# A three-stage attention and gated-MLP kernel: the half pair in the first group of the sixth-stage products, the second group run backward, four weight sets converted later and in place

## The chip, the cores and the metric

The kernel runs on one core of a Trainium2 chip. The core has five engines with a queue each: PE (TensorE, matmuls; PEld is its weight load), DVE (VectorE), ACT (ScalarE), POOL (GpSimd) and SP (SyncE, which here issues nearly all DMAs). The metric is the device time of one execution in microseconds (us), less is better.

## What is computed

Attention over 32 learned slots (8 batches, 8 heads, 576 tokens, 64 wide), then a gated MLP, then a squared-ReLU MLP:

```python
x = attention(q, k, v, phi)                    # 4608 tokens x 512
xn = x / sqrt(mean(x * x) + 1e-6) * rms_g
y = (silu(xn @ w_gate) * (xn @ w_val)) @ w_out1   # 512 -> 1536 -> 512
h = maximum(y @ w_in2, 0) ** 2                 # 512 -> 2048
out = h @ w_out2                               # 2048 -> 512
```

## The kernel before

Every fp32 product is made of three fp32r matmuls: each operand is split into a high part (a rounded copy, ACT) and a low part (the rest, DVE or POOL), and high x high, high x low and low x high are summed in PSUM. The helper `split` (L76) does this; it is the line behind most ACT rows (L79) and DVE or POOL rows (L88, and L100 where the low part is put off to the next piece).

**Phase A** (`phase_a`, L886) makes attention and the gated MLP, batch by batch, 24 items (n) a batch: an item is half a batch (288 tokens) by 128 of the 1536 hidden columns. PE makes g and v (6 matmuls each), ACT makes Silu of g (`sl`, L898), DVE multiplies by v, ACT and POOL split the product (`uh`, `ul`), and two items later PE multiplies it by `w_out1` into y (24 matmuls an item in all). g has one PSUM bank: PE cannot begin g of item n+1 before ACT has read g of item n. Each item has four slots, a (after g), b (after v), c (after `uh`), d (after the products into y), where other work is put in program order.

**The last batch** (items 168 to 191) has no next batch's attention to prepare. There the slots from n = 171 on take one piece each from a list (`last_batch`, L921). The pieces prepare the last MLP, which is made by a Strassen-like scheme of 7 products for 8: `x2` pieces (seven each for two halves kk of the tokens of one pair) make the seven sums of y blocks, split; `w2` pieces make the seven sums of a weight block: two pieces with sums on POOL (`w2_sums`), three that split 256, 512 and 1024 columns (`w2_split`, parts a, c, b; ACT, then DVE). A finished weight set is 128 x 3584 fp32 (1792 KB) and is stored to DRAM (`wd`). The input of a set is 512 KB (two DMAs, into `xr`, which has two buffers, and from there the next is loaded when the last piece of a set has run). There are eight sets of `w_in2` ("i", q = 0 to 7) and eight of `w_out2` ("z"). In the last batch all eight z sets and i sets 0 and 1 are made.

**Phase H** (`phase_h`, L1140) makes h. A step is a pair of token blocks by a set q: seven products, 42 matmuls, 512 columns wide (256 in the half pair, pair 4), with four results `c` that are squared and stored to `gd`. `c` has six buffers. Pairs 0 and 2 keep their sums in the `x0` tiles, 1 and 3 in `x1`, the half pair in `x4`. The order of the steps is written out in `STEPS` (L42): group 0 has pairs 0 and 1 (A, B), group 1 pairs 2, 3 and 4 (A, B, C), both with q from 0 up. `h_plan` (L1085) tells which pieces and loads go with which step. In group 0 the i sets 2 to 7 are made, stored, and all eight are loaded again (`Wr`, L1006) for group 1, in three slots `wi0`, `wi1`, `wi2`, the load a step to three ahead of its use. In the last steps of group 1 the eight z sets are loaded (`T`, L1013) into the freed `x0` and `x1` tiles.

**Phase Z** (`phase_z`, L1247) makes out: 72 sums g, 42 matmuls each, from the z sets and from sums S of h. For each g, `s_load` loads two blocks (`sr`, 2 x 256 KB), `s_sums` adds on DVE and POOL, `s_split` makes S (1792 columns: ACT 1.7 us, DVE 2 us) in the `wi` slots. S of g = 0 and 1 are made in group 1; `sr` of g = 2 goes into `x4_1`, that of g = 3 into `xr`. Every four sums share four PSUM accumulators; the first four take the banks y0 to y3.

The DMAs of SP go out in program order, and land about in that order when the queue is full.

Of the kernel before, what the change touches and what calls it, by code (L numbers as in the profile page):

```python
# [9 lines left out]
F32 = mybir.dt.float32  # L10
# [44 lines left out]

TOK = (0, P, HALF - P)
# [8 lines left out]
class Kernel:  # L65
# [88 lines left out]
    def run(self):  # L154
# [43 lines left out]
        with tc.manual_schedule():  # L198
            self.phase_a(NI * (B - 1) + 3, NI * B + 1)
# [721 lines left out]
    def last_batch(self):  # L921
# [61 lines left out]
    def w2_split(self, kind, q, slot, part):  # L983
# [101 lines left out]
    def h_plan(self):  # L1085
# [3 lines left out]
        def at(g, name, pieces, *loads):  # L1089
            p = 2 * g + "ABC".index(name[0])  # L1090
# [8 lines left out]
        def w2(q):  # L1099
            return self.w2_pieces("i", q, q % 3)  # L1100
# [10 lines left out]
        at(0, "B1", w2(3), wl(5))
        at(0, "A3", w2(4), xl(4, 0))
        at(0, "A4", w2(5), wl(6))
        at(0, "B3", x2(4, 0), xl(4, 1))
        at(0, "A5", w2(6), wl(7))
        at(0, "B4", x2(4, 1), xl(2, 0))
        at(0, "A6", w2(7), xl(2, 1))
        at(0, "B5", x2(2, 0, 0, 5))
        at(0, "B6", x2(2, 0, 5), xl(3, 0))
        at(0, "B6", x2(2, 1, 0, 3))  # L1120
        at(0, "B7", x2(2, 1, 3), xl(3, 1))
        at(1, "A0", x2(3, 0, 0, 5))
        at(1, "A1", x2(3, 0, 5), partial(self.s_load, 0))
# [229 lines left out]
```

## Time and profile before

| | |
|---|---|
| median of 3 runs | 1628.73 us (1628.13 to 1630.13) |
| profiled execution | 1628.44 us, span of its instructions 1626.7 us |
| busy: PE, DVE, ACT, POOL | 94%, 63%, 45%, 39% |
| chain that ended last | PE 72%, DVE 8%, DMA 6%, ACT 5%, POOL 4% |
| HBM read, written | 208.28 MB, 101.84 MB |

Times in the rows are counted from the start of the span. Phase A ends near 886 us, its last batch takes about the last 110 us of it; phase H runs from 886 to 1242, its group 1 from 1045; phase Z from there to the end. PE is the engine that does the work, so the question at each place is what it waits for, and which of its two clock levels was granted. A busy PE in the profile includes some waiting, since the ends of matmuls are modelled.

### The profile page before, as it was taken

The page shows a single profiled execution, that of the slowest core. Times are in us where ns is not written, and L with a number is a line of the kernel's source. Part 1 is how long each engine was busy: PE and PEld are TensorE (multiplying, and loading weights), DVE is VectorE, ACT ScalarE, POOL GpSimd, SP SyncE. Part 2 cuts the span into 40 slices and gives each one's busy share as a digit, 9 for nine tenths or more (in the row PEclk, how much of TensorE's full clock was granted, in tenths as well). Part 3 has the DMA queues.
Part 4 walks back from the last instruction along what each step waited for, and adds up shares of the span by engine and source line. Part 5 has one row for each costly group of instructions (what it writes and reads, how often), then busy time and mean ns, then how long its engine had stood idle before and what let it go on. Part 6 is the DMA issues. An engine that isn't in the chain of part 4 may idle for free.

```text
span 1626.7 us, 29659 instructions
## 1 busy us (share of the span) xinstructions
PE 1530.5 (94%) x11594; PEld 1353.6 (83%) x11594; DVE 1016.8 (63%) x1548; ACT 733.0 (45%) x1304; POOL 639.6 (39%) x637
## 2 busy tenths in 40 slices
PE   6687999999999999999878999999998899999998
PEld 3465798888989888898877788878887899999998
DVE  5755645656464565635644777776654777777874
ACT  2656535354443545434543656664443333333332
POOL 0475534344344434424564513430000444444442
PEclk7788999999999999999989999999998899999999
DMA  9897583764758374313496577866479444444442
GB/s 264 278 313 257 205 231 137 211 197 148 189 188 230 132 216 145 111 52 132 151 345 227 196 257 266 265 205 232 164 249 333 144 130 130 138 138 134 135 130 69
DMA packets 207388, 312.07 MB, mean 192 GB/s; under 512 B 31664, under 2 KB 151472, under 8 KB 197008
## 3 DMA queue, kind: packets, MB, share of 16 engines
q1 hardware_dynamic: 203360, 307.56, 58.4%
q10 hardware_dynamic: 3824, 2.49, 0.6%
q8 instruction: 91, 1.49, 0.4%
q14 instruction: 49, 0.40, 0.1%
q0 software_dynamic: 64, 0.13, 0.0%
HBM read 208.28 MB, written 101.84 MB: 191 GB/s over the span
## 4 chain that ended last, share of the span: by engine, by line
PE 72%; DVE 8%; DMA 6%; ACT 5%; POOL 4%; issue 4%; SPq 0%; DVEq 0%; POOLq 0%; ACTq 0%
PE z L1277 7%; PE z L1275 7%; PE z L1276 7%; PE y L868 5%; PE y L869 5%; PE y L870 5%; PE v L852 3%; PE h_S L1082 3%; PE h_S L1083 3%; PE h_S L1081 3%; PE wp L571 3%; PE g L852 3%; PE v L853 2%; PE v L854 2%; PE g L853 2%
## 5 line engine op out<-in xcount | busy, mean ns | idle before, releaser
L88 POOL TENSOR_TENSOR ul<-sl,uh 128x288 fp32r<-128x288 f32 x192 | 168.7, 879 | 365.8 <-ACT uh L79 361.4
L1275 PE MATMUL z<-T,S 128*128 128x256 f32 x1008 | 286.8, 285 | 12.8 <-ACT S L79 6.0
L1277 PE MATMUL z<-T,S 128*128 128x256 f32 x1008 | 286.1, 284 | 1.3 <-DVE S L88 1.3
L1276 PE MATMUL z<-T,S 128*128 128x256 f32 x1008 | 286.0, 284 | 0.0
L868 PE MATMUL y<-uh,woh 128*128 128x288 f32 x768 | 237.1, 309 | 0.0
L869 PE MATMUL y<-uh,wol 128*128 128x288 f32 x768 | 229.1, 298 | 0.0
L870 PE MATMUL y<-ul,woh 128*128 128x288 f32 x768 | 227.9, 297 | 0.0
L79 ACT ACTIVATE S<-sr 128x1792 fp32r<-128x1792 f32 x72 | 122.6, 1703 | 205.4 <-PE z L1277 141.4
L902 DVE TENSOR_TENSOR sl<-sl,v 128x288 f32<-128x288 f32 x192 | 86.0, 448 | 199.4 <-PE v L854 141.0
L1275 PEld LDWEIGHTS z<-T,S 128*128 128x128 f32 x1008 | 195.2, 194 | 13.5 <-ACT S L79 6.2
L1277 PEld LDWEIGHTS z<-T,S 128*128 128x128 f32 x1008 | 194.1, 193 | 1.6 <-DVE S L88 1.6
L1276 PEld LDWEIGHTS z<-T,S 128*128 128x128 f32 x1008 | 194.2, 193 | 0.0
L88 DVE TENSOR_TENSOR S<-sr,S 128x1792 fp32r<-128x1792 f32 x70 | 144.0, 2057 | 55.8 <-ACT S L79 55.8
L1231 POOL TENSOR_TENSOR sr<-sr 128x256 f32<-128x256 f32 x72 | 84.1, 1168 | 232.3 <-DVE sr L1228 232.3
L868 PEld LDWEIGHTS y<-uh,woh 128*128 128x128 f32 x768 | 146.6, 191 | 18.0 <-issue 17.2
L79 ACT ACTIVATE uh<-sl 128x288 fp32r<-128x288 f32 x192 | 85.1, 443 | 158.3 <-DVE sl L902 157.4
L852 PE MATMUL g<-anh,wph 128*128 128x288 f32 x384 | 121.5, 316 | 32.6 <-ACT sl L898 29.9
L898 ACT ACTIVATE sl<-g 128x288 f32<-128x288 f32 x192 | 78.2, 407 | 159.3 <-PE g L854 151.3
L869 PEld LDWEIGHTS y<-uh,wol 128*128 128x128 f32 x768 | 146.8, 191 | 0.7
L870 PEld LDWEIGHTS y<-ul,woh 128*128 128x128 f32 x768 | 146.5, 191 | 0.0
L1167 ACT ACTIVATE c<-c 128x512 f32<-128x512 f32 (+1 forms) x120 | 70.1, 584 | 150.0 <-DVE c L1193 96.3
L1229 POOL TENSOR_TENSOR sr<-sr 128x256 f32<-128x256 f32 x72 | 77.6, 1078 | 133.0 <-DMA sr<-gd 123.9
(192 smaller groups left out, 3775.2 us busy)
## 6 DMA issues: line engine op xcount, KB each, us to landing
w<-w SPq DMA_DIRECT2D x48, 1024.0 KB, 6.8
sr<-gd SPq DMA_DIRECT2D x144, 256.0 KB, 3.4
gd<-c SPq DMA_DIRECT2D x128, 256.0 KB, 2.9
q<-in_q_dram SPq DMA_DIRECT2D x128, 144.0 KB, 5.6
wdz<-Wz SPq DMA_DIRECT2D x8, 1792.0 KB, 6.9
wdi<-Wi SPq DMA_DIRECT2D x8, 1792.0 KB, 7.0
Wr<-wdi SPq DMA_DIRECT2D x8, 1792.0 KB, 8.2
T<-wdz SPq DMA_DIRECT2D x8, 1792.0 KB, 9.2
```

What stands on the lines that cost most here:

```text
L79: nc.scalar.activation(hi, src, AF.Copy)
L88: f()
L852: nc.tensor.matmul(out, wh[:, r, cs], ah[:, r], start=(r == 0), stop=False)
L868: nc.tensor.matmul(y, hi[:, cs], uh, start=first, stop=False)
L869: nc.tensor.matmul(y, lo[:, cs], uh, start=False, stop=False)
L870: nc.tensor.matmul(y, hi[:, cs], ul, start=False, stop=last)
L898: nc.scalar.activation(sl, gp, AF.Silu)
L902: nc.vector.tensor_tensor(sl, sl, vp, op=ALU.mult)
L1231: nc.gpsimd.tensor_tensor(t[:, 7], t[:, 2], t[:, 5], op=ALU.subtract)
L1275: nc.tensor.matmul(out, sh, th, start=first, stop=False, **kw)
L1276: nc.tensor.matmul(out, sh, tl, start=False, stop=False, **kw)
L1277: nc.tensor.matmul(out, sl, th, start=False, stop=last, **kw)
```

## The change

The half pair (4) goes from group 1 to group 0, so group 0 has three pairs (0, 1, 4 as A, B, C) and group 1 two (2, 3). Group 1 runs q from 7 down to 0: it begins with the sets 7, 6, 5 that group 0 left in the three slots, and loads sets 4 to 0 alone. Of the z sets only 4 to 7 are made and stored in the last batch, with i sets 2, 0 and 1; z sets 0 to 3 are made in group 1 straight in the tiles where phase Z reads them, and neither stored nor loaded. i sets 5 to 7 are not stored. The pieces of the last batch begin one item earlier (n = 170) and go into slots c and d, and into a only where the next piece is a `w2_sums`. The first four sums of phase Z take the banks g, v and att instead of y0 to y3, and `sr` of g = 2 goes into `x1_2`.

```diff
+PAIRS = ((0, 1, 4), (2, 3))
+W_SLOT, S_SLOT = (1, 0, 2), (2, 0, 1)
+T_SLOT = ("x4_0", "x4_1", "x0_0", "x0_1", "x0_2", "x0_3", "x1_0", "x1_1")
-        ("AB", 0, "A0A1A2B0B1A3B2A4B3A5B4A6A7B5B6B7"),
-        ("ABC", 2, "A0A1A2B0C0B1C1A3B2C2A4B3C3A5B4C4A6A7B5C5B6B7C6C7"),
+        ("ABC", PAIRS[0], "A0A1A2B0B1C0B2C1A3C2B3A4C3B4A5C4B5A6A7B6B7C5C6C7"),
+        ("AB", PAIRS[1], "A7A6A5B7B6A4B5A3B4A2B3A1A0B2B1B0"),
+LAST = 2
-        if n >= NI * (B - 1) + 3:
+        if n >= NI * (B - 1) + LAST and (pos in "cd" or pos == "a" and self.side and self.side[0].func == self.w2_sums):
             self.piece()
-        for q in range(1, NQ):
-            after = load("z", q + 2) if q < NQ - 2 else load("i", q + 2 - NQ)
-            out += then(self.w2_pieces("z", q, q % 2), after)
-        out += then(self.w2_pieces("i", 0, 0), partial(self.x2_load, 1, 0))
-        out += then(self.w2_pieces("i", 1, 1), load("i", 2))
+        jobs = [("z", 5, 1), ("z", 6, 0), ("z", 7, 1), ("i", 2, 0), ("i", 0, 1), ("i", 1, 0)]
+        for i, (kind, q, slot) in enumerate(jobs):
+            after = load(*jobs[i + 2][:2]) if i + 2 < len(jobs) else partial(self.x2_load, 1, i + 2 - len(jobs))
+            out += then(self.w2_pieces(kind, q, slot), after)
-            self.after(partial(self.nc.sync.dma_start, self.wd[kind, q], t.bitcast(F32)))
+            if q < 5 if kind == "i" else q > 3:
+                self.after(partial(self.nc.sync.dma_start, self.wd[kind, q], t.bitcast(F32)))
...
+        at(1, "B6", [partial(self.wi_load, 4)] + tw(0)[:2])
+        at(1, "A4", [partial(self.wi_load, 3)] + tw(0)[2:], tl(2))
...
+        at(1, "A1", [partial(self.wi_load, 0)])
+        at(1, "A0", tw(3)[:2])
+        at(1, "B2", tw(2)[2:], partial(self.s_load, 0))
+        at(1, "B2", tw(3)[2:], partial(self.s_load, 1))
+        at(1, "B1", [partial(self.wt_load, 4), partial(self.wt_load, 5)] + self.s_sums(0) + self.s_split(0))
+        at(1, "B0", self.s_sums(1) + self.s_split(1))
-        for f in [partial(self.s_load, 2), partial(self.s_load, 3)] + self.s_sums(2):
+        for f in [partial(self.wt_load, 6), partial(self.s_load, 2), partial(self.wt_load, 7), partial(self.s_load, 3)] + self.s_sums(2):
-                    for i, tag in enumerate((("y0", "y1", "y2", "y3"), ("g", "v", "att", "att"))[run % 2])
+                    for i, tag in enumerate((("g", "v", "att", "att"), ("y0", "y1", "y2", "y3"))[run % 2])
```

ACT's queue in the last batch, before: `sl` is Silu of an item (its number in the name), `uh` the high part of its product, `Wz` the splits of a z set.

```order
L898 ACTIVATE sl177_9858<-g177_9849 128x288
L79 ACTIVATE uh177_9875<-sl177_9858 128x288
L79 ACTIVATE Wz2_9893<-sz2_9814 128x256
L79 ACTIVATE Wz2_9893<-sz2_9814 128x512
L898 ACTIVATE sl178_9904<-g178_9895 128x288
L79 ACTIVATE Wz2_9893<-sz2_9814 128x1024
L79 ACTIVATE uh178_9916<-sl178_9904 128x288
L79 ACTIVATE Wz3_9948<-sz3_9871 128x256
L898 ACTIVATE sl179_9950<-g179_9941 128x288
```

The same queue after, at the sets of z 6 and 7:

```order
L902 ACTIVATE sl182_10038<-g182_10029 128x288
L83 ACTIVATE uh182_10048<-sl182_10038 128x288
L83 ACTIVATE Wz6_10052<-sz6_9939 128x256
L83 ACTIVATE Wz6_10052<-sz6_9939 128x512
L902 ACTIVATE sl183_10079<-g183_10072 128x288
L83 ACTIVATE uh183_10089<-sl183_10079 128x288
L83 ACTIVATE Wz6_10052<-sz6_9939 128x1024
L902 ACTIVATE sl184_10123<-g184_10114 128x288
L83 ACTIVATE uh184_10133<-sl184_10123 128x288
L83 ACTIVATE Wz7_10137<-sz7_10026 128x256
```

A set took five slots of four an item before; now it takes exactly two items, and no split stands between an item's Silu and its `uh`.

SP's queue where group 1 loads weight sets again, before, at the end of step C4 and in A6 (set 7 is read in A7, the next step):

```order
L1171 DMA gd4_4_9562<-c12_4_4_13190 128x256
L1171 DMA gd4_4_9562<-c21_4_4_13168 128x256
L1006 DMA Wr7_13214<-wdi7_9517 128x3584
L1171 DMA gd2_6_9548<-c11_2_6_13223 128x512
L1171 DMA gd2_6_9548<-c22_2_6_13254 128x512
```

The same queue after, at the end of step B7 and in B6 (set 4 is read in A4, the next step):

```order
L1184 DMA gd3_7_9520<-c12_3_7_12819 128x512
L1184 DMA gd3_7_9520<-c21_3_7_12797 128x512
L1010 DMA Wr4_12843<-wdi4_9477 128x3584
L1184 DMA gd3_6_9519<-c11_3_6_12852 128x512
L1184 DMA gd3_6_9519<-c22_3_6_12887 128x512
```

Sets 4 and 0 are now loaded one step ahead, as set 7 was; sets 3, 2 and 1 two steps ahead.

SP's queue at the end of phase H and the start of Z, before (`sr2` is the input of g = 2):

```order
L1013 DMA T6_13757<-wdz6_9524 128x3584
L1171 DMA gd4_7_9565<-c11_4_7_13766 128x256
L1013 DMA T7_13771<-wdz7_9525 128x3584
L1171 DMA gd4_7_9565<-c22_4_7_13802 128x256
L1171 DMA gd4_7_9565<-c12_4_7_13814 128x256
L1171 DMA gd4_7_9565<-c21_4_7_13791 128x256
L1216 DMA sr2_13829<-gd0_4_9530 128x4x128
L1216 DMA sr2_13829<-gd0_5_9531 128x4x128
L1216 DMA sr3_13832<-gd0_6_9532 128x4x128
```

The same place after:

```order
L1184 DMA gd3_0_9513<-c12_3_0_13791 128x512
L1184 DMA gd3_0_9513<-c21_3_0_13768 128x512
L1016 DMA T6_13806<-wdz6_9487 128x3584
L1229 DMA sr2_13808<-gd0_4_9493 128x4x128
L1229 DMA sr2_13808<-gd0_5_9494 128x4x128
L1016 DMA T7_13811<-wdz7_9488 128x3584
L1229 DMA sr3_13813<-gd0_6_9495 128x4x128
```

Six loads of z sets that stood in the last steps are gone or earlier; T6 now stands ahead of `sr2`, and T7 between `sr2` and `sr3`.

## Rows read from the trace of the kernel before

**Rows 1.** Page, part 2: granted clock in tenths, 40 slices of 40.7 us.

```profile
PEclk7788999999999999999989999999998899999999
```

**Rows 2.** Windows, phase A's last batch: window, length, busy us (instructions) per engine, PE clock, DMA share, GB/s.

```profile
775.00:800.00 25.00, 22.95 (x174) 22.22 (x167) 14.61 (x24) 13.24 (x28) 11.97 (x12) 1.00 0.42 128
800.00:825.00 25.00, 20.87 (x131) 19.00 (x131) 17.56 (x26) 13.00 (x26) 17.13 (x16) 0.93 0.71 262
825.00:850.00 25.00, 18.01 (x109) 16.84 (x107) 11.54 (x16) 11.00 (x22) 15.09 (x19) 0.86 0.97 353
850.00:875.00 25.00, 18.87 (x110) 17.84 (x111) 11.17 (x14) 9.49 (x20) 14.38 (x18) 0.86 0.93 328
```

**Rows 3.** Timeline of ACT, last batch: start, us; Silu of items 170, 177, 188, 190, 191.

```profile
781.78 0.39 ACT L898 ACTIVATE sl<-g 128x288 f32<-128x288 f32 x1
...
813.43 0.39 ACT L898 ACTIVATE sl<-g 128x288 f32<-128x288 f32 x1
...
871.00 0.39 ACT L898 ACTIVATE sl<-g 128x288 f32<-128x288 f32 x1
...
877.41 0.41 ACT L898 ACTIVATE sl<-g 128x288 f32<-128x288 f32 x1 [1.45 <-PE g L854]
...
880.62 0.41 ACT L898 ACTIVATE sl<-g 128x288 f32<-128x288 f32 x1 [1.47 <-PE g L854]
```

**Rows 4.** Waits of PE, 760 to 1627 us: total us, times, longest us.

```profile
PE g L852 <- ACT sl L898: 17.2, 9, 4.6
PE z L1275 <- ACT S L79: 6.0, 1, 6.0
PE z L1275 <- DVE c L1193: 5.1, 1, 5.1
PE h_S L1082 <- DVE x L100: 2.9, 2, 2.1
PE h_A L1081 <- DMA Wr<-wdi: 1.9, 2, 1.2
...
PE z L1275 <- DVE c L1198: 1.7, 1, 1.7
PE z L1277 <- DVE S L88: 1.3, 1, 1.3
```

**Rows 5.** Chain that ended last, last batch, one loop of a weight set: start, us, what.

```profile
832.73 1.07 ACT Wz L79
...
835.07 0.32 SPq L100
835.55 7.48 DMA sz<-w_z
...
847.36 1.06 ACT Wz L79
```

**Rows 6.** The same chain in phase H, step A6, and z set loads on the page, part 6.

```profile
1180.24 8.29 DMA Wr<-wdi
...
T<-wdz SPq DMA_DIRECT2D x8, 1792.0 KB, 9.2
```

**Rows 7.** Timeline of DVE at the start of phase Z: start, us; idle before in brackets.

```profile
1251.62 0.42 DVE L1198 TENSOR_TENSOR c<-h_S,u 128x256 f32<-128x256 f32 x1 [4.17 <-DMA gd<-c]
...
1264.72 0.42 DVE L1227 TENSOR_TENSOR sr<-sr 128x256 f32<-128x256 f32 x1 [11.88 <-DMA sr<-gd]
...
1266.56 0.53 DVE L1227 TENSOR_TENSOR sr<-sr 128x256 f32<-128x256 f32 x1 [0.56 <-DMA sr<-gd]
...
1268.57 2.08 DVE L88 TENSOR_TENSOR S<-sr,S 128x1792 fp32r<-128x1792 f32 x1 [0.61 <-ACT S L79]
```

**Rows 8.** Windows at the start of phase Z, columns as in rows 2.

```profile
1240.00:1244.00 4.00, 2.36 (x21) 2.15 (x19) 1.40 (x5) 3.29 (x6) 0.00 (x0) 1.00 0.94 287
...
1272.00:1276.00 4.00, 4.00 (x21) 4.00 (x21) 3.11 (x3) 1.47 (x1) 3.40 (x2) 0.50 0.55 163
...
1300.00:1304.00 4.00, 4.00 (x36) 4.00 (x35) 3.72 (x5) 1.42 (x2) 0.75 (x1) 1.00 0.29 76
```

More of the change, by code (lines that the diff above doesn't have):

```diff
@@ L41 @@
 W_ORDER = ("A11", "A12", "A22", "S1", "S2", "S3", "S4")
+PAIRS = ((0, 1, 4), (2, 3))
+W_SLOT, S_SLOT = (1, 0, 2), (2, 0, 1)
+T_SLOT = ("x4_0", "x4_1", "x0_0", "x0_1", "x0_2", "x0_3", "x1_0", "x1_1")
 STEPS = [
-    [(p, int(q)) for name, q in zip(names[::2], names[1::2]) for p in [order.index(name) + base]]
-    for order, base, names in (
-        ("AB", 0, "A0A1A2B0B1A3B2A4B3A5B4A6A7B5B6B7"),
-        ("ABC", 2, "A0A1A2B0C0B1C1A3B2C2A4B3C3A5B4C4A6A7B5C5B6B7C6C7"),
+    [(p, int(q)) for name, q in zip(names[::2], names[1::2]) for p in [pairs[order.index(name)]]]
+    for order, pairs, names in (
+        ("ABC", PAIRS[0], "A0A1A2B0B1C0B2C1A3C2B3A4C3B4A5C4B5A6A7B6B7C5C6C7"),
+        ("AB", PAIRS[1], "A7A6A5B7B6A4B5A3B4A2B3A1A0B2B1B0"),
     )
@@ L184, in run @@
             self.prologue()
-            self.phase_a(0, NI * (B - 1) + 3)
+            self.phase_a(0, NI * (B - 1) + LAST)
         for cm in reversed(cms):
@@ L930, in load @@
             return partial(self.w2_load, kind, q)
-        out = [partial(self.chain, partial(self.x2_load, 0, 0), load("z", 0))]
-        out += then(x2(0), partial(self.x2_load, 0, 1)) + then(self.w2_pieces("z", 0, 0), load("z", 1))
-        out += then(x2(1), load("z", 2))
-        for q in range(1, NQ):
-            after = load("z", q + 2) if q < NQ - 2 else load("i", q + 2 - NQ)
-            out += then(self.w2_pieces("z", q, q % 2), after)
-        out += then(self.w2_pieces("i", 0, 0), partial(self.x2_load, 1, 0))
-        out += then(self.w2_pieces("i", 1, 1), load("i", 2))
+        out = [partial(self.chain, partial(self.x2_load, 0, 0), load("z", 4))]
+        out += then(x2(0), partial(self.x2_load, 0, 1)) + then(self.w2_pieces("z", 4, 0), load("z", 5))
+        out += then(x2(1), load("z", 6))
+        jobs = [("z", 5, 1), ("z", 6, 0), ("z", 7, 1), ("i", 2, 0), ("i", 0, 1), ("i", 1, 0)]
+        for i, (kind, q, slot) in enumerate(jobs):
+            after = load(*jobs[i + 2][:2]) if i + 2 < len(jobs) else partial(self.x2_load, 1, i + 2 - len(jobs))
+            out += then(self.w2_pieces(kind, q, slot), after)
         return out
@@ L1111, in h_plan @@
[L1111 to L1123, printed above, removed]
@@ L1134, in h_plan @@
-        at(1, "B6", self.s_sums(0))
-        at(1, "B7", self.s_split(0))
-        at(1, "C6", self.s_sums(1))
-        at(1, "C7", self.s_split(1))
+        at(0, "A0", [partial(self.wi_load, 2)] + x2(1, 0, 0, 5))
+        at(0, "A1", x2(1, 0, 5), xl(4, 0))
+        at(0, "A1", x2(1, 1, 0, 3))
+        at(0, "A2", x2(1, 1, 3), xl(4, 1))
+        at(0, "B0", x2(4, 0), wl(3))
+        at(0, "B1", x2(4, 1), wl(4))
+        at(0, "C0", w2(3)[:2])
+        at(0, "B2", w2(3)[2:], wl(5))
+        at(0, "C1", w2(4)[:2])
@@ new lines, in h_plan @@
+        at(0, "A3", w2(4)[2:], wl(6))
+        at(0, "C2", w2(5)[:2])
+        at(0, "B3", w2(5)[2:], wl(7))
+        at(0, "A4", w2(6)[:2])
+        at(0, "B4", w2(6)[2:], xl(2, 0))
+        at(0, "A5", w2(7)[:2])
+        at(0, "B5", w2(7)[2:], xl(2, 1))
+        at(0, "B6", x2(2, 0), xl(3, 0))
+        at(0, "B7", x2(2, 1), xl(3, 1))
+        at(1, "A7", x2(3, 0, 0, 5))
+        at(1, "A6", x2(3, 0, 5), tl(0))
+        at(1, "A6", x2(3, 1, 0, 3))
+        at(1, "A5", x2(3, 1, 3), tl(1))
+        at(1, "B6", [partial(self.wi_load, 4)] + tw(0)[:2])
@@ L1213, in s_load @@
         else:
-            t = self.wb2.tile([P, 8, 2, P], F32, tag="x4_1", name=f"sr{g}")
+            t = self.wb2.tile([P, 8, 2, P], F32, tag="x1_2", name=f"sr{g}")
         for i in range(2):
```

41 lines of the change are left out of this document (18 added, 23 removed).

## The prediction, made before the changed kernel ran

> **What bounds the kernel now.** I read the granted clock in the page's slices first, then windows of busy time, then PE's waits and, at each place where PE waits, the chain and the queues there. The clock is full over most of the span, with dips in slices 20 to 22 and around slice 31 [rows 1]. The first is the last batch. In its four windows PE is idle for 2.1, 4.1, 7.0 and 6.1 us, at a clock of 0.86 to 1.00, and the DMA share climbs to 0.97 [rows 2]. PE's longest wait is for Silu on ACT, 17.2 us [rows 4]: Silu stands in ACT's queue behind the splits of the weight sets. An undisturbed item takes 3.21 us (877.41 to 880.62). From item 170 to 191 there are 21 items, 67.4 us; they took 98.84 [rows 3]. So **31.4 us are lost in the last batch**: 9.2 up to item 177 (31.65 us for 7 items), where the `x2` pieces stand, and 22.3 from there to item 188 (57.57 us for 11 items), where nine weight sets are made.
>
> What paces those sets is a loop through one input buffer: split on ACT, store and next load, landing 7.48 us after the load's issue, sums on POOL, next split: 832.73 to 847.36, 14.6 us, with two buffers 7.3 us a set [rows 5].
>
> The second dip is the start of phase Z. PE's last matmul of phase H ends at 1242.4 (2.36 us into its window) [rows 8]. PE then waits 5.1 and 1.7 us for DVE to free the accumulators y0 to y3, and 6.0 and 1.3 us for S of g = 2 [rows 4]. DVE itself waited for a store of `c` (4.17 us) and for `sr` (11.88 us), both queued behind set loads; the low part of S is done at 1270.65 [rows 7]. The first two sums, 84 matmuls at 36 in 4 us, need 9.3 us, so 19.0 us are idle or slow up to there; the third sum then runs at half clock (21 matmuls in 4 us), some 2.7 us more [rows 8]. That is **21.7 us lost**.
>
> In phase H itself PE waits little: 2.9 us for `x2` low parts and 1.9 us for `Wr` loads, the longest 1.2 [rows 4].
>
> **Part 1, the last batch.** Ten weight sets become seven, and a piece goes only into c and d (sums into a as well). By the order of ACT's queue a set takes two items, 6.4 us of matmuls, where 1.25 items gave it 4.0 us before. The `x2` pieces, two an item instead of four, ask less of DVE and ACT than an item offers; I put 1 us on them, for the first load, which stands right ahead of its first piece. The sets: z 4, 5 and 6 find their inputs landed, since these are loaded during the `x2` pieces. The other four hang on the loop: z 5, z 7, i 0 and z 6, i 2, i 1, two turns each. A turn takes 14.6 us [rows 5] and the order offers four items, 12.8: 1.8 us late a turn, 3.7 in two turns, and 1.6 more because item 181 has no product into y. Against this stands slack: between g of one item and g of the next lie 18 matmuls of 0.134 us (3.21 by 24), 2.4 us, less Silu's 0.4, so Silu may be 2.0 us late before PE waits. 3.7 + 1.6 - 2.0 + 1 = 4.4 us lost, **27.0 us gained**. No wait is then long, so I take the clock as full. The bounds: nothing lost gives 31.4; the same loss a set as before (22.3 by nine is 2.5, for six sets 15) and the 9.2 of the `x2` pieces kept give 24 lost, 7.4 gained. I stay near the upper end, since the loop's row is a measured one and only its pace against the items is new.
>
> **Part 2, phase H.** The number of matmuls stays, and I take their pace as unchanged. The set i 2, made in A1 before, is now loaded at A0 and needed two steps, some 20 us, later; a load lands after 8.3 us [rows 6]. The sums of pair 1 end in the middle of A2 instead of at its end, so the 2.9 us go. New are three places. Sets 4 and 0 are loaded one step ahead, just as set 7 was before, whose load (8.29 us) made PE wait 1.2 us [rows 4, 6]: 2.4 us for both. The half pair's sums end in B1, right ahead of C0: 0.4 us, DVE's last low part behind its two other operations. What waits behind the load on SP is a store of `c`, and of these there are six buffers. The z sets 0 to 3 made in group 1 have as many columns each as an S, which takes DVE 2.08 us [rows 7], in steps of 9.9 us (phase H's 356 us by 32 full and 8 half steps); only B2, with two sets, is full. 4.8 lost becomes 2.8: **2 us gained**, between 5 gained and 4 lost (each of the two loads as late again as here, and B2 late by 1).
>
> **Part 3, the start of phase Z.** The accumulators are now g, v and att, which the last step's first products leave early: the 6.8 us go. `sr` of g = 2 still cannot start before the last matmul of H, since `x1_2` is read to the end, and T6 stands ahead of it. Count from that matmul: SP issues T6 at about 2.0 (two DVE operations and a store's issue are ahead). T6 with `sr2` behind it is as large as a set's store with the next input behind, which land 8.0 us after the store's issue [rows 5]: 10.0. T7 and `sr3` are the same again at 7.3 a round: 17.3. Now the order on DVE: the sums of g = 3 stand ahead of the low part of S of g = 2. Before, `sr3` landed right behind `sr2`, and that cost nothing; now T7 lies between. From those sums to the end of the low part are 4.1 us (1266.56 to 1270.65) [rows 7]: 21.4. PE needs it at 9.3: 12.1 us idle, and 2.7 for half clock as before. 14.8 against 21.7: **7 us gained**. Bounds: if `sr3` does not hold the low part back, it is done 5.9 us after `sr2` [rows 7], at 15.9, and 12.4 us are gained; if set loads take the 9.2 us of before [rows 6], 1.2 more each, 4.5; if S comes as late as before, nothing.
>
> Against the rows stands a fit of the Trainium skill (DMA: Bandwidth & Descriptors, Anatomy of one DMA): 2.0 us and the bytes by 436 GB/s, an estimate of 6.2 us for 1792 KB; the row has 8.29, so the trace does not agree. By the fit the round of T6 and `sr2` is an estimated 7.4 and the next 5.4, S would come 2.5 us earlier and a loop of part 1 would be 0.6 shorter, some 1588.5 in all.
>
> **The sum.** 27 + 2 + 7 = 36 us. From the profiled execution, 1628.44 us (0.3 below the median of the runs, span 1626.7), this gives 1592.4: **1592 us**.
>
> **The rivals.** *The last batch stays paced by its sets.* If a set loses 2.5 us as before, six lose 15, with 1 for `x2` 16 of 31.4; 15.4 are gained there instead of 27, and the time is 1604. For it: DMA at 0.97 [rows 2], and two items a set still ask for 2.3 MB in 6.4 us, more than the 353 GB/s seen there. Against it: three inputs land early, and the slack of 2 us.
>
> *The start of phase Z gains nothing.* S comes as late as before, for T6 and T7 both stand ahead of what it needs. Against it: six of the eight loads no longer lie there. 1599.
>
> *Slower: results back up in the half steps of group 0.* A half step makes four results in 4.9 us into six buffers. Where stores queue behind set transfers, DVE waits as it did at the end of phase H (4.17 us [rows 7]) and PE 6.8 [rows 4]. At all eight half steps that is 54 us, against 36 gained: 1646. It decides from about six such steps on. For it: group 0 now carries the half steps and set stores together. Against it: only two sets are stored there, and the queue was this deep only when set loads followed each other.
>
> *The gains are real but cancel*, by half clock after new waits: within 0.2%, about 1628.
>
> That the change does less than it says is not open: the queues' order shows the sets, loads and pieces as described.
>
> **How the numbers follow.** Forecast 0.64, the paced last batch 0.17, phase Z without gain 0.12, the half steps 0.05, cancelled 0.02. The lowest time is all three upper bounds, 31.4 + 5 + 12.4: 1580. Upward the range takes in both milder rivals and half of what they cost together (1611), 1608. **Range 1580 to 1608.** 0.2% is about what a measurement can tell from no change: faster 0.93, same 0.02, slower 0.05.
>
> **What would show it.** In the changed profile: from Silu of item 170 to that of 191 about 72 us instead of 98.8, no window there under a clock of 0.95, and PE's wait for Silu near 5 us; two waits of some 1.2 us for `Wr` in group 1, at A4 and A0; at phase Z no wait for `c`, and one of about 12 us for S of g = 2, the DVE waiting for `sr3` ahead of it. A last batch at 84 us, or PE waits for DVE in the half steps, would prove it wrong.

## The result, and the profile after

| | before | after |
|---|---|---|
| median, first comparison | 1628.43 us (1627.44 to 1630.13) | 1611.55 us (1610.60 to 1612.06) |
| ratio, 95% interval | | 0.9895 (0.9877 to 0.9912) |
| median, second comparison | 1627.64 us | 1607.82 us, ratio 0.9883 (0.9868 to 0.9898) |
| profiled execution, span | 1628.44, 1626.7 us | 1612.06, 1610.2 us |
| HBM read, written | 208.28, 101.84 MB | 197.27, 89.00 MB |

The change gains 17 us in the first comparison and 20 in the second, where the prediction had 36 (1592, range 1580 to 1608). The sign was right, the size about half.

To see where the rest went, the span is cut at four places that can be read in the timelines: Silu of item 170, the last product into y (end of phase A), the last matmul of phase H, and the start of phase Z's seventh sum, from which on Z runs without a wait. In us of one profiled execution each:

| | last batch | phase H | start of Z | rest of Z |
|---|---|---|---|---|
| before | 104.0 | 356.3 | 50.7 | 327.3 |
| after, first comparison | 81.3 | 364.7 | 49.3 | 326.9 |
| after, second comparison | 78.8 | 365.3 | 48.6 | 326.9 |
| gained, measured | 22.8 to 25.2 | -8.4 to -9.0 | 1.4 to 2.1 | 0.4 |
| gained, predicted | 27.0 | 2 | 7 | 0 |

Up to item 170 the code is the same in all kernels here, and yet that item came at 777.7 to 783.2 us in the profiles of the changed kernel and its variants: 5 us of difference between single executions have nothing to do with any edit. The table by stage leaves them out, and the experiments below are read from it first and from the medians second.

The clock in the page's slices, against [rows 1]:

```profile
PEclk7798999999999999999999999999999899999999
```

Counted from 1, [rows 1] has its second dip in slice 21 alone (the last batch; the prediction's "20 to 22" is a misreading) and its third in 31 and 32 (the start of Z). The second is gone, of the third one slice is left. The windows of the last batch, against [rows 2] (window, length, busy us (instructions) per engine, PE clock, DMA share, GB/s):

```profile
775.00:800.00 25.00, 24.36 (x182) 23.97 (x181) 15.24 (x24) 12.52 (x29) 11.14 (x13) 1.00 0.32 98
...
825.00:850.00 25.00, 23.67 (x172) 22.60 (x170) 12.49 (x18) 12.17 (x25) 16.81 (x21) 1.00 0.92 342
850.00:875.00 25.00, 22.54 (x114) 19.64 (x115) 13.56 (x18) 10.61 (x21) 10.30 (x11) 0.93 1.00 349
```

PE is busy for 23.7 to 24.9 of 25 us at full clock up to 850, where it had 18.0 to 22.9 before. PE's waits from 760 us on, against [rows 4] (total us, times, longest):

```profile
PE z L1288 <- ACT S L83: 11.3, 1, 11.3
PE z L1290 <- DVE S L92: 4.8, 1, 4.8
PE h_S L1084 <- ACT x L83: 3.4, 1, 3.4
PE y L874 <- POOL ul L92: 3.2, 3, 2.2
PE h_A L1084 <- DMA Wr<-wdi: 3.2, 2, 2.6
PE h_S L1085 <- DVE x L104: 1.4, 1, 1.4
PE h_S L1084 <- DVE c L1192: 1.3, 1, 1.3
...
PE g L856 <- ACT sl L902: 0.2, 1, 0.2
```

Of the 17.2 us for Silu 0.2 are left, and the 6.8 for the accumulators (L1193 and L1198 of before) are gone. In their place stand one long wait for S of g = 2 (16.1 us, high and low part, instead of 7.3) and, in phase H, waits that were not there, for an `x2` high part on ACT and for results on DVE, and one for a `Wr` load that was 1.2 us and is 2.6.

In phase H three places cost more than a step without waits (9.5 to 9.8 us for a full one, 4.8 to 5.0 for a half one; durations from one step's first matmul to the next one's): **C0** 11.9 us, 7.0 too many (6.7 in the second profile); **C5 to C7** 4.4 too many (7.5, with the step A7 behind them); **B6 with A4** 12.5 and 11.2, 4.4 too many (2.0). The step ahead of A0 adds 0.6 (1.1). Against these 16.4 us (17.3) 8.1 of before went: 4.9 at A2 and B0, 2.0 in the first steps of group 1, 1.2 for set 7. Windows over C0 (two), A4 (one) and the start of Z, columns as above:

```profile
912.00:916.00 4.00, 0.64 (x7) 0.44 (x5) 2.86 (x6) 3.13 (x7) 3.84 (x7) 0.82 0.18 66
916.00:920.00 4.00, 2.61 (x10) 2.31 (x11) 2.96 (x5) 1.30 (x4) 1.58 (x2) 0.50 0.46 171
...
1120.00:1124.00 4.00, 4.00 (x14) 3.19 (x13) 0.66 (x1) 0.60 (x1) 0.00 (x0) 0.65 1.06 316
...
1252.00:1256.00 4.00, 1.35 (x6) 1.35 (x7) 3.97 (x4) 0.79 (x1) 3.64 (x3) 0.50 0.01 3
1256.00:1260.00 4.00, 4.00 (x23) 4.00 (x22) 3.36 (x4) 2.60 (x2) 1.70 (x3) 0.59 0.43 130
```

Behind each of these waits the clock is lower. It is 0.50, the lower of its two levels, at 916 and at 1252, and 0.65 on average at 1120, where PE is busy for all of 4.00 us and gets 14 matmuls done; a window without waits has 18 or 19.

### The profile page after: what moved, and what is told of

Its sections match the earlier page's. It is cut to its first block, busy times and chain, and to the rows that moved or that the text cites. A ratio compares the mean times of both kernels' runs of the same rounds, so it can differ in the third digit from the quotient of the medians.

```text
span 1610.2 us, 29592 instructions
## 1 busy us (share of the span) xinstructions
PE 1522.1 (95%) x11594; PEld 1348.3 (84%) x11594; DVE 1014.0 (63%) x1548; ACT 732.9 (46%) x1304; POOL 638.3 (40%) x637
## 3 DMA queue, kind: packets, MB, share of 16 engines
HBM read 197.27 MB, written 89.00 MB: 178 GB/s over the span
## 5 line engine op out<-in xcount | busy, mean ns | idle before, releaser
L1288 PE MATMUL z<-T,S 128*128 128x256 f32 x504 | 142.5, 283 | 11.3 <-ACT S L83 11.3
L1242 POOL TENSOR_TENSOR sr<-sr 128x256 f32<-128x256 f32 x72 | 79.1, 1098 | 184.7 <-DMA sr<-gd 184.7
L1290 PE MATMUL z<-T,S 128*128 128x256 f32 x504 | 142.3, 282 | 4.8 <-DVE S L92 4.8
L1289 PE MATMUL z<-T,S 128*128 128x256 f32 x504 | 142.3, 282 | 0.0
L1288 PE MATMUL z<-Wz,S 128*128 128x256 f32 x504 | 142.0, 282 | 0.0
L1290 PE MATMUL z<-Wz,S 128*128 128x256 f32 x504 | 141.9, 282 | 0.0
L1289 PE MATMUL z<-Wz,S 128*128 128x256 f32 x504 | 141.9, 282 | 0.0
L856 PE MATMUL g<-anh,wph 128*128 128x288 f32 x384 | 119.0, 310 | 14.5 <-ACT sl L902 11.9
L856 PE MATMUL v<-anh,wph 128*128 128x288 f32 x384 | 119.8, 312 | 3.4 <-DVE sl L906 3.3
```

Of the source, the lines that this page charges most:

```text
L856: nc.tensor.matmul(out, wh[:, r, cs], ah[:, r], start=(r == 0), stop=False)
L1242: nc.gpsimd.tensor_tensor(t[:, 4], t[:, 0], t[:, 3], op=ALU.add)
L1288: nc.tensor.matmul(out, sh, th, start=first, stop=False, **kw)
L1289: nc.tensor.matmul(out, sh, tl, start=False, stop=False, **kw)
L1290: nc.tensor.matmul(out, sl, th, start=False, stop=last, **kw)
```

## The experiments

Each is one edit to the changed kernel, where nothing else is said. The tests come in the order of phase H, phase Z, last batch. The changed kernel ran a second time in one comparison, to stand beside three of them:

> The changed kernel as it is, beside the next three on the same chip, so that they are compared with it there. 1611 again. The first trace of it lost 397 us from the middle of item 165 on to the last product into y, three variants with the same code up to there 395: theory (the wait for ul at the end of the last batch varies from run to run, 1.6 to 3.7 us), a value between the two; rival (it is fixed), 397.

Measured: 1607.82 us. (The stretch named there begins earlier than the text says, near item 85; cut at item 170 it is 81.3 and 78.8 us.) The last batch takes 78.8, as in all later variants with the same code there (78.5 to 79.5). The 81.3 of the first profile is the outlier. PE's waits for `ul` from item 170 on add up to 2.7 us here (the longest 1.4) and 3.2 there (2.2), and the clock behind the last of them, from 858 to 862, was 0.74 there and stayed at 1.00 here.

### Phase H: the first half step, C0

```diff
-"A0A1A2B0B1C0B2C1A3..."
+"A0A1A2B0B1B2C0C1A3..."
```

> The changed kernel with one edit: the first half step C0 stands after B2 instead of ahead of it (B1 B2 C0 C1 instead of B1 C0 B2 C1), so a full step without x2 pieces lies between the 28 x2 pieces of A0 to B1 and the first half step; the pieces of w2 set 3 move with it (sums in B2, splits in C1). In the changed kernel C0 takes 11.9 us where a half step without waits takes 4.95. Theory (ACT and DVE carry a backlog of 3 to 4 us out of the x2 pieces, which a full step of 9.8 us of matmuls would absorb): C0 near 5 us, 6 to 7 us gained, about 1605. Rival (a half step has too little matmul time for its own relu, square and stores, whatever stands before it): the loss moves with C0, and two half steps in a row lose more; 1611 or above.

Measured: 1602.08 us, ratio 0.9839 (0.9819 to 0.9860). C0 takes 4.95 us and PE is busy for 4.00 of 4 us in all windows from 900 to 928, here over the end of C0 and the start of C1:

```profile
920.00:924.00 4.00, 4.00 (x36) 4.00 (x36) 3.06 (x8) 2.45 (x7) 1.66 (x2) 1.00 0.64 231
```

Phase H is 6.8 us shorter (358.5 against 365.3). The theory holds, the half step itself is not the trouble. (Two pieces with sums of weight set 3 moved away with it; they run on POOL, and neither of PE's waits at C0 was for POOL.) What was behind it is seen in the changed kernel's ACT timeline just ahead of C0 (start, us, operation; idle before in brackets):

```profile
912.81 0.63 ACT L1180 ACTIVATE c<-c 128x512 f32<-128x512 f32 x1 [2.00 <-DVE c L1206]
...
914.00 0.40 ACT L83 ACTIVATE x<-xr 128x256 fp32r<-128x256 f32 x1
...
915.49 0.71 ACT L83 ACTIVATE x<-xr 128x256 fp32r<-128x256 f32 x2
```

and in DVE's:

```profile
910.23 0.42 DVE L104 TENSOR_TENSOR x<-xr,x 128x256 fp32r<-128x256 f32 x1 [0.74 <-ACT x L83]
...
911.36 0.69 DVE L1204 TENSOR_TENSOR u<-h_S,u 128x512 f32<-128x512 f32 x1
912.08 0.69 DVE L1206 TENSOR_TENSOR c<-h_S,u 128x512 f32<-128x512 f32 x1
```

B1 runs on PE from 900.9 to 910.7, seven products of 1.4 us; the fifth, which L1204 reads, was done at 907.9, 3.4 us before DVE came to it. DVE waits for high parts on ACT, ACT waits for results on DVE with the next high part queued behind them, and so both fell behind through the 28 pieces of A0 to B1. The last high parts of the half pair, at 915.49, are what PE waits for.

### Phase H: set 4 of group 1

```diff
-"A7A6A5B7B6A4B5A3B4A2..."
+"A7A6A5B7B6B5A4A3B4A2..."
```

> The changed kernel with one edit: in group 1, B5 stands ahead of A4 (B6 B5 A4 A3 instead of B6 A4 B5 A3), so the load of set 4, issued at B6, has two steps instead of one before A4; set 3 is loaded at B5, set 2 at A4, and the pieces of the z sets move with them. In the changed kernel PE waits 2.6 us for set 4 (load 7.9 us from issue to landing), A4 takes 4.4 us more than a step without waits, part of it at half clock. Theory: the wait and the half clock behind it both go, 4 to 4.5 us, about 1607. Rival (only the wait goes and the clock falls anyway, or set 3 or 2 becomes late in turn): 2 us or less, 1609.5 or above.

Measured: 1604.47 us, ratio 0.9856 (0.9833 to 0.9879); phase H 360.5 us, 4.8 shorter than the second profile of the changed kernel. B5, A4 and A3 take 9.5 to 9.6 us each, PE is busy all through, here over the end of B5 and the start of A4:

```profile
1116.00:1120.00 4.00, 4.00 (x19) 3.30 (x18) 3.93 (x6) 2.19 (x3) 0.00 (x0) 1.00 0.93 373
```

Wait and half clock both go. Of the 4.8 us, 2.0 are what the wait of that profile cost, the others came at C5 to C7, which were better in this execution and which the edit does not touch. Why the wait was longer than the 1.2 us of before is seen on SP (start, us from the first issue to the last):

```profile
1103.74 6.81 SPq L1184 DMA_DIRECT2D gd<-c  x5
1110.64 0.40 SPq L1010 DMA_DIRECT2D Wr<-wdi  x1
```

B6 starts at 1106.14. The load stands behind the stores of B7's last results and goes out 4.5 us into the step; 7.9 us later it lands, 12.4 after the start of a step of 9.8. In the second profile it goes out 3.4 us into B6 and PE waits 1.8. Before, set 7 went out 2.6 us into its step.

### Phase H: the last half steps

```diff
-"...A6A7B6B7C5C6C7"
+"...A6C5A7C6B6B7C7"
```

> The changed kernel with one edit: the last three half steps of group 0 are spread (A6 C5 A7 C6 B6 B7 C7 instead of A6 A7 B6 B7 C5 C6 C7). In the changed kernel C5 takes 0.5 us and C6 4.0 us more than a half step without waits, at a clock of 0.58 for a part. Theory (three half steps in a row ask more of DVE, ACT and the six result buffers than their 15 us of matmuls hide): the 4.5 us go, about 1607. Rival (it is the 14 x2 pieces of B6 and B7 ahead of them, as with C0): C7 right behind B7, or A7 behind it, now loses as much as before, 1611 or above.

Measured: 1612.78 us, ratio 0.9916 (0.9899 to 0.9933): nothing gained, the median is 5 us above the changed kernel's in the same comparison. The two profiled executions differ by 2.3 (1608.91 and 1606.60), and those lie ahead of item 170; the rest is seen in no trace. By steps the half steps did what the theory said: C5 and C6 lose nothing, C7 0.7 and A7 behind it 1.1, together 5.7 us less than the second profile's 7.5. It came back in group 1: B7 loses 1.7 (the `x2` pieces of pair 3 are later), and PE waits 4.2 us for set 4, where it was 1.8:

```profile
PE h_A L1084 <- DMA Wr<-wdi: 4.2, 1, 4.2
```

So the loss of C5 to C7 is real, but taking it away alone is worth nothing while set 4 stands where it does. Phase H is as long as it was (365.1).

### The start of Z: accumulators alone

The kernel before with one part of the change: `("g", "v", "att", "att")` as the first accumulators.

> The kernel before with one part of the change alone: the first accumulators of phase Z are g, v and the two att banks, the second ones y0 to y3. In the kernel before PE waits 6.8 us for DVE to free y0 to y3 and then 7.3 us for S of g = 2. Theory (both waits hang on the same queue of loads, and the second one takes up what the first one gives): the wait for S grows by nearly as much, 0 to 1 us gained, 1628. Rival (as the prediction's sum had it, the accumulators' wait goes in full): 6 to 7 us gained, 1622.

Measured: 1627.69 us against 1627.81, ratio 1.0000 (0.9990 to 1.0009). The accumulators' waits are gone, and the wait for S has become 16.3 and 1.3 us, where [rows 4] had 6.0 and 1.3:

```profile
PE z L1275 <- ACT S L79: 16.3, 1, 16.3
PE z L1277 <- DVE S L88: 1.3, 1, 1.3
```

The later wait took all of it, as the theory said.

### The start of Z: the order of the loads

```diff
-[wt_load(6), s_load(2), wt_load(7), s_load(3)]
+[s_load(2), s_load(3), wt_load(6), wt_load(7)]
```

> The changed kernel with one edit: at the start of phase Z the loads of sr for g = 2 and 3 are issued ahead of the set loads T6 and T7 (before: T6, sr2, T7, sr3). In the changed kernel SP issues T6 7.3 us after phase H's last matmul, sr2 has landed at +17.6, sr3 at +23.8, and the low part of S of g = 2 is done at about +27.1, where PE needs it at +9.3. Theory (the order of the queue holds S back): sr2 lands near +11, sr3 near +12, the low part of S is done near +17.5; some 9.5 us less idle there, about 1602. Rival (the late issue on SP and the split of S of g = 1 set it, the loads of T cost little because both kinds share the 16 DMA engines anyway): the low part of S comes no more than 3 us earlier, 1609 or more, and T6 becomes late for the fourth sum.

Measured: 1603.97 us, ratio 0.9846 (0.9828 to 0.9864). The low part of S of g = 2 was done 17.7 us after the end of phase H's last matmul, as the theory had it (17.5), but the start of Z was only 2.9 us shorter than in the second profile. DVE's timeline shows the rest:

```profile
1239.25 2.01 DVE L92 TENSOR_TENSOR S<-sr,S 128x1792 fp32r<-128x1792 f32 x1
1249.33 0.42 DVE L1240 TENSOR_TENSOR sr<-sr 128x256 f32<-128x256 f32 x1 [8.07 <-DMA sr<-gd]
...
1250.54 2.01 DVE L92 TENSOR_TENSOR S<-sr,S 128x1792 fp32r<-128x1792 f32 x1
```

The sums of g = 4 stand ahead of the low part of S of g = 3, and `sr` of g = 4 now lay behind T6 and T7. What the prediction said of `sr3` came true one sum later. So the next edit put `sr4` ahead of T6 and T7 too:

```diff
-[wt_load(6), s_load(2), wt_load(7), s_load(3)]
+[s_load(2), s_load(3)], and wt_load(6), wt_load(7) behind s_load(4)
```

> The changed kernel with one edit: SP issues sr for g = 2, 3 and 4 ahead of T6 and T7 at the start of phase Z. With only sr2 and sr3 ahead, S of g = 2 came 9.3 us earlier, but 3.5 us were gained: sr of g = 4 landed behind T6 and T7, 26 us after phase H's end, and its sums stand ahead of the low part of S of g = 3 on DVE, so PE waited for that instead. Theory (the same order on DVE, one sum later): with sr4 ahead too, only S of g = 2 is waited for, at +17.5 to +18.5; 8 to 9 us gained against the changed kernel, about 1599.5. Rival (T6 and T7, needed by the fourth sum, are now late themselves, or sr5 takes the part of sr4): 4 us or less, 1604.

Measured: 1599.73 us, ratio 0.9829 (0.9808 to 0.9849); start of Z 41.1, 7.6 us less than in the second profile, and one wait is left:

```profile
PE z L1291 <- ACT S L83: 6.0, 1, 6.0
PE z L1293 <- DVE S L92: 1.3, 1, 1.3
```

T6 and T7, issued behind six `sr` loads, are not waited for. The theory holds.

The other way to undo that order, on DVE instead of SP, is to put the split of g + 2 ahead of the sums of g + 3:

```diff
-side = self.s_sums(g + 3) + self.s_split(g + 2)
+side = self.s_split(g + 2) + self.s_sums(g + 3)
```

> The changed kernel with one edit: in phase Z the split of S for g + 2 stands ahead of the sums for g + 3 on DVE, instead of behind them. In the changed kernel DVE waits 4.9 us for sr of g = 3 with the low part of S of g = 2 queued behind that wait, while S's high part is ready at 1249. Theory (the order on DVE is one of three causes of the wait there, beside the late issue and T6 ahead of sr2): PE's wait for the low part, 4.8 us, goes nearly in full, the wait for the high part stays, 3 to 4 us gained, 1607.5. Rival (sr3 lands with the next wait behind it anyway, so the third sum only waits later): under 1 us, 1611.

Measured: 1635.55 us, ratio 1.0046 (1.0030 to 1.0061). Neither theory had this. The start of Z did get shorter, 45.7 against 48.6, but the rest of Z took 356.5 us instead of 326.9: 66 sums of 5.4 us instead of 5.0. One round there, from the timeline of DVE, POOL and ACT:

```profile
1408.19 0.42 DVE L1241 TENSOR_TENSOR sr<-sr 128x256 f32<-128x256 f32 x1
...
1408.69 0.74 POOL L1244 TENSOR_TENSOR sr<-sr 128x256 f32<-128x256 f32 x1 [3.97 <-DVE sr L1241]
...
1409.46 1.71 ACT L83 ACTIVATE S<-sr 128x1792 fp32r<-128x1792 f32 x1 [3.70 <-POOL sr L1244]
...
1411.20 2.02 DVE L92 TENSOR_TENSOR S<-sr,S 128x1792 fp32r<-128x1792 f32 x1 [2.59 <-ACT S L83]
```

With the split first, sums, POOL's difference, high part and low part of every sum form one ring, from DVE's first sum at 1407.74 to that of the next g at 1413.14, 5.4 us, and PE asks for a sum each 5.0. With the sums first, DVE works on g + 3 while ACT splits g + 2, and the ring is cut. The order that costs 3 us once at the start is worth 30 us afterwards.

### The start of Z: why T6 is issued late

The prediction had T6 issued 2.0 us after phase H's last matmul, it was 7.3. In the changed kernel's DVE timeline the split of S of g = 1 stands ahead of the last results of B0:

```profile
1228.05 2.02 DVE L104 TENSOR_TENSOR S<-sr,S 128x1792 fp32r<-128x1792 f32 x1 [1.57 <-ACT S L83]
...
1245.17 0.42 DVE L1240 TENSOR_TENSOR sr<-sr 128x256 f32<-128x256 f32 x1 [11.85 <-DMA sr<-gd]
...
1251.37 0.42 DVE L1240 TENSOR_TENSOR sr<-sr 128x256 f32<-128x256 f32 x1 [4.91 <-DMA sr<-gd]
...
1252.58 2.01 DVE L92 TENSOR_TENSOR S<-sr,S 128x1792 fp32r<-128x1792 f32 x1
```

The last results of B0 come to DVE from 1230.0 on, SP issues T6 at 1234.8. The edit takes the split out of the way:

```diff
-at(1, "B0", s_sums(1) + s_split(1))
+at(1, "B0", s_sums(1) + [four empty pieces] + s_split(1))
```

> The changed kernel with one edit: the split of S of g = 1 stands behind all seven products of the last step B0 instead of behind the third. In the changed kernel that split (1.7 us on ACT, 2.0 on DVE) stands ahead of B0's last results, so SP, which stores them in order, issues T6 7.3 us after phase H's last matmul, where the prediction had 2.0. Theory (the split makes T6 late, and all that follows with it): T6 is issued at about +3.5, S of g = 2 comes 3.5 to 4 us earlier, 1604 beside the 1608 of the changed kernel in the last comparison. Rival (S of g = 1 now becomes late for the second sum, or the loads meet B0's stores and land no earlier): 1 us or less, 1607.

Measured: 1609.38 us, ratio 0.9886 (0.9868 to 0.9905), no gain. T6 went out at +5.6 instead of +7.3. With the split out of the way, DVE waited for a result buffer instead:

```profile
1229.93 0.69 DVE L1211 TENSOR_TENSOR c<-h_S,u 128x512 f32<-128x512 f32 x1 [2.12 <-DMA gd<-c]
```

The stores of B1 stand behind T4 and T5 on SP and land 7.7 to 11.4 us after their issue. Two covers, then. What they are worth was still open:

```diff
-at(1, "B1", [wt_load(4), wt_load(5)] + ...)
+at(1, "B2", [wt_load(4), wt_load(5)] + ...)
```

> The changed kernel with one edit: SP issues the set loads T4 and T5 in B2 instead of B1 (both of phase H's end; their room is free from A0 on). In the changed kernel the results of B1 stand behind them on SP and land 7.7 to 11.4 us after issue instead of 2.3. With the split of S of g = 1 moved out of the way DVE waited 2.1 us for such a store, so there are two covers of the same 5 us. Theory: with the split still ahead of B0's results this edit alone brings under 2 us, 1606. Rival (the stores behind T4 and T5 are the whole cause): T6 is issued at about +3, 4 us gained, 1604.

> The changed kernel with both edits, T4 and T5 in B2 and the split of S of g = 1 last. Theory (two covers, the split and the stores behind T4 and T5): no wait of DVE for a store in B0, T6 issued at +2.5 to +3 after phase H's last matmul as the prediction had it, S of g = 2 4 us earlier, of which the late split of g = 1 gives back 1: 1604 to 1605. Rival (a third thing holds SP, for instance the loads of sr0 and sr1 in B2): T6 still at +5 or later, 1608.

Measured: 1615.02 us, ratio 0.9925 (0.9907 to 0.9942), and with the split last 1611.39, ratio 0.9908 (0.9893 to 0.9922). In the second one T6 goes out at +4.1: DVE no longer waits for a store in B0, and what stands between DVE and SP in the timeline is ACT, with relu and square of the last two results. So of the 5.3 us beyond the predicted 2.0 the split made 1.7 and the stores 1.5; that ACT makes the other 2.1 is read from the timeline and was not tested. But neither edit brings time. With T4 and T5 in B2, `sr0` is late, its sums hold up the results of B1 on DVE, and B0 takes 14.2 and 14.4 us instead of 9.8 (the line is from the profile with both edits):

```profile
1213.51 0.43 DVE L1240 TENSOR_TENSOR sr<-sr 128x256 f32<-128x256 f32 x1 [4.19 <-DMA sr<-gd]
```

Phase H is 4 to 5 us longer for it (369.5 and 370.1). Moved one step ahead, the loads cost as much as they did.

### The last batch: fewer sets or sparser pieces

```diff
-if n >= ... and (pos in "cd" or pos == "a" and <next piece is a sum>):
+if n >= ...:
```

> The changed kernel with one edit: in the last batch the pieces stand in all four places of an item again, as in the kernel before, with the seven sets of the change instead of ten. The changed kernel needs 73.6 us from the Silu of item 170 to that of 191, the kernel before 98.8. Theory of the prediction (both parts count: with two items a set the loop through the input buffers no longer makes Silu wait, with 1.25 it does): seven sets in the old places lose about 2.5 us each again after the first three, some 10 us of the 24 are lost, 1621. Rival (three sets fewer are the whole gain, since the last item's place is free for the rest): within 3 us of the changed kernel.

Measured: 1629.72 us, ratio 1.0013 (1.0002 to 1.0023): 22 us slower than the changed kernel in the same comparison, back at the kernel before, with seven sets instead of ten. 17.3 of these lie in the batch, which takes 96.2 us instead of 78.8, and PE waits for Silu again:

```profile
PE g L856 <- ACT sl L902: 12.3, 7, 4.1
```

The prediction's theory had the direction, with 10 us, less than half; three sets fewer leave 7.8 of the 25 us, and 17 need the sparser places.

### Together

C0 later, the half steps spread, B5 ahead of A4, `sr2` to `sr4` ahead of T6 and T7, the split of g = 1 last; then the same with `sr3` loaded in B0; then also with T4 and T5 in B2:

> The changed kernel with five edits together: C0 later, the last half steps of group 0 spread, B5 ahead of A4 in group 1, sr2 to sr4 ahead of T6 and T7, the split of S of g = 1 last. If the places are independent, the gains add: C0 6.5, the half steps 3, the Wr4 wait 4, the start of Z 8.5 and the split 3.5, 25 us from 1608: 1583. Rival (what is gained in phase H comes back as lost at the next place, since the clock or the queues give part of it back): 1592 or above.

> As the five edits together, and sr of g = 3 is loaded in the last step B0, where its buffer is free, so that at the start of phase Z only sr2 and sr4 stand ahead of T6. Theory (the first load of the queue counts most): 1 to 2 us less than the five edits, 1581.5. Rival (sr3 ahead of B0's stores delays them and with them sr2): the same or 1 us more.

> The six edits together (C0 later, half steps spread, B5 ahead of A4, sr2 and sr4 ahead of T6 and T7, the split of S of g = 1 last, sr3 in B0), and T4 and T5 in B2. In the six edits DVE waits 2.5 us for a store in B0. Theory: this wait goes, 2 to 3 us less, 1583. Rival (the load of sr2 is then held by something else): the same 1585.5.

Measured: 1589.25 us (ratio 0.9759, 0.9737 to 0.9782), **1585.59 us (0.9741, 0.9722 to 0.9759)** and 1589.72 (0.9772, 0.9752 to 0.9793). The sums made beforehand, 1583, 1581.5 and 1583, were 4 to 7 us too low. By stages 352.2, 352.3 and 357.4 for phase H, 40.8, 38.4 and 37.1 for the start of Z. Phase H gains 13.1 us; of the 17.3 us counted above, 4.1 are left (C7 0.7, A7 1.1, B7 1.7, the step ahead of A0 0.6). So the half steps' 5.7 us, worth nothing alone, count as soon as set 4 is out of the way, less the 1.7 that B7 loses for them: 4.0. The start of Z gains 7.8, hardly more than the load order alone, so the late split of g = 1 adds nothing there either. `sr3` in B0 brings another 2.4 at the start of Z, T4 and T5 in B2 take 5.2 in phase H for 1.3. The second one is the fastest version, 22 us below the changed kernel. The two largest items of its waits (total, times, longest):

```profile
PE y L874 <- POOL ul L92: 3.1, 3, 1.7
PE z L1293 <- DVE S L92: 2.7, 2, 1.9
```

## Why the prediction missed, point by point

Of the 36 us forecast 18 came. Most of the other 18 lies in three costs of phase H (C0, set 4 and C5 to C7) and in one time at the start of phase Z (the issue of T6).

- **Part 1 had the size right, and the path of what is left wrong.** 27.0 us predicted, 25.2 measured (22.8 in the first profile). Silu of item 170 to that of 191 took 72.1 us (73.6), about 72 was forecast. That the waits for Silu go is right, and the dense version shows that the places of the pieces make them go. But the 4.4 us that the sum left as lost (its terms add up to 4.3) were Silu coming late behind the loop of the sets, a wait near 5 us, and PE waited 0.2 us for Silu. About as much, 4.7 us (6.2), is lost otherwise: at item 175 PE waits 0.6 us for DVE to read v, and from item 186 on 1.2 us for `ul` on POOL (second profile); what makes the rest is open. So that 72 came out is in part luck. The 2 us missing stand behind item 191: `ul` of the last item waits on POOL behind the sums of set i 1, whose input came late, and PE waits up to 2.2 us for it, which the sum did not have:

```profile
854.62 0.73 POOL L975 TENSOR_TENSOR si<-si 128x256 f32<-128x256 f32 x1 [3.94 <-DMA si<-w_i]
...
857.67 1.55 POOL L92 TENSOR_TENSOR ul<-sl,uh 128x288 fp32r<-128x288 f32 x2
```

  The rival of a paced batch is what the dense version shows (91.0 us from 170 to 191), not the changed kernel.
- **Part 2 had the wrong sign: 2 us gained predicted, 8.4 to 9.0 lost.** Its gains came, and larger than counted: A2 and B0 of before had lost 4.9 us, at a clock of 1.00, where the sum had 2.9. PE's waits there were 2.5 us for `x2`, and 1.1 for the new set i 2, which the sum left out; the other 0.8 of the 2.9 stood in group 1, whose first steps gave 2 more. The costs failed in three terms. *C0 at 0.4 us* cost 7.0. The term took the last piece's own place in DVE's queue; it did not ask how far ACT and DVE were behind by then, with 28 pieces in the five steps ahead and a half step of 4.9 us next. C0 later shows it. *Set 4 at 1.2 us*: PE waited 2.6 us and lost 4.4, with the lower clock behind the wait (in the second profile 1.8 and 2.0). "One step ahead, as set 7 was" was the wrong measure: set 7 went out 2.6 us into its step, set 4 goes out 4.5 (3.4) into it, behind the stores of the step before. Set 0, the other one, fits (0.6 to 1.1). *C5 to C7* were not in the sum at all, 4.4 to 7.5 us. They are the rival of results backing up in the half steps, at three of eight half steps, those that follow each other behind the 14 `x2` pieces of B6 and B7, but not by its path, stores behind set transfers. C5 began on PE at 1048.6, and its first result came to DVE only at 1057.3, behind `x2` low parts:

```profile
1055.04 2.36 DVE L104 TENSOR_TENSOR x<-xr,x 128x512 fp32r<-128x512 f32 x2
1057.32 0.41 DVE L1192 TENSOR_TENSOR c<-h_A,p 128x256 f32<-128x256 f32 x1
```

  In the second profile DVE then also waited for a store, issued behind six loads for the `x2` pieces of pair 3 and landed 4.5 to 4.8 us later, where the next stores of that size take 1.7 to 1.8:

```profile
1060.42 0.42 DVE L1206 TENSOR_TENSOR c<-h_S,u 128x256 f32<-128x256 f32 x1 [3.19 <-DMA gd<-c]
```

- **Part 3 had the mechanism and missed its start.** 7 us predicted, 1.4 to 2.1 measured. The accumulators' wait went in full, as predicted, and the order on DVE is as described: 4.91 us for `sr3` with the low part of S of g = 2 behind it. The failed step is T6's issue at +2.0, which was +7.3. The rounds behind it were near in sum: T6 and `sr2` landed 10.2 after T6's issue (8.0 predicted), `sr3` 6.2 later (7.3), and the sums and the low part took 3.2 (4.1); that these three errors nearly cancel is luck. Taking that one term as measured turns the 14.8 us into 20.1 and the 7 into 1.6. "Two DVE operations and a store's issue" left out the split of S of g = 1, which the diff puts into B0, the stores behind T4 and T5, and ACT's relu and square. Neither the split alone, nor the loads moved alone, nor both brought a gain; ACT's part was not tested. What the runs do show is that the order of the queue is worth 7.6 us: with `sr2` to `sr4` ahead of T6 and T7 the start of Z fell to 41.1.
- **Against the fit.** The text beside part 3 had 6.2 us for a set by the Trainium skill (DMA: Bandwidth & Descriptors, Anatomy of one DMA), and that the trace did not agree. The Trainium skill gives this fit for DMAs of the gpsimd path, and here SP issues them. It does not agree here either: the five loads of group 1 took 7.9 to 10.1 us, and the profile's median of all six `Wr` loads is 8.4.

```profile
Wr<-wdi SPq DMA_DIRECT2D x6, 1792.0 KB, 8.4
```

- **The sum.** 25 - 9 + 2 is 18, against 17 to 20 measured. 36 became 18 by 11 us in part 2, 5 in part 3 and 2 in part 1. The range's upper end, 1608, took in the milder rivals of parts 1 and 3. The first did not come. The second, that S comes as late as before because T6 and T7 stand ahead of what it needs, came in the main, at a chance of 0.12: the low part of S of g = 2 was done 26.9 us after phase H's end, where it had been 28.3. Part 2's lower bound, 4 us lost, was half of what happened, and its own terms, two loads each 1.2 us later and B2 1 us, make only 1.4: the new places were priced from rows in which the engines were on time.

## What to carry to other kernels

A wait priced from a queue's tail holds only if the engines are on time when it is reached: ahead of a short step, count how much the queues are behind after all the pieces before it, and give them a long step to catch up. A transfer's lead is counted from where its issue stands in its queue, behind the stores of the step before, not from the step's name. At a place where several things are late by the same few us, taking one away shows the next; the edit worth making is the one that reorders the queue (`sr` ahead of T: 7.6 us), and an order that hurts once at the start may be what keeps the steady part fast.

## What the runs showed of the hardware

- **The clock after a wait.** At C0 two waits, 3.4 and 1.4 us, cost 7.0 us: the clock was 0.50 in the window of 916 to 920, behind the first wait. At A4 a wait of 2.6 us was followed by a window at 0.65, and one of 4.2 us, in the kernel with the half steps spread, by one at 0.58. Behind 1.8 us at A4 in the second profile the clock was full, and so it was in step B0 of before, behind waits of 2.1 and 0.4 us (at 1116 the second profile's window, at 924 that of before):

```profile
1116.00:1120.00 4.00, 4.00 (x20) 3.30 (x19) 1.38 (x2) 1.90 (x4) 0.00 (x0) 1.00 1.06 308
...
924.00:928.00 4.00, 4.00 (x19) 3.22 (x18) 3.37 (x6) 1.26 (x2) 1.82 (x3) 1.00 0.57 197
```

  The sum of idle time does not tell it either: in the dense last batch PE was idle for 6.2 of 25 us at a clock of 1.00, and in the next 25 us for 6.8 at 0.86.

```profile
800.00:825.00 25.00, 18.84 (x126) 17.02 (x126) 15.19 (x22) 11.57 (x24) 17.59 (x17) 1.00 0.73 257
825.00:850.00 25.00, 18.16 (x114) 17.63 (x114) 12.14 (x17) 10.52 (x22) 14.74 (x18) 0.86 0.99 366
```

- **A store behind two set loads.** A 256 KB store of `c` lands 2.3 us after its issue when SP's queue is empty; behind T4 and T5 the same store took 7.7 to 11.4 us.
